# Score products of cosine attention in eight quarter tiles instead of two halves, from the second batch on

## The chip, the core and the metric

The kernel runs on one core of one Trainium2 chip, as one program. The core has a matrix engine (TensorE, PE in the profile, with its weight loads listed apart as PEld), a vector engine (DVE), a scalar engine that evaluates functions (ACT), GpSimd (POOL), and SyncE (SP), which here only issues transfers; transfers run on 16 DMA engines. The metric is the device time of one execution in microseconds, taken as the median of several runs.

## What is computed

Cosine attention, followed by two matrix products with a leaky ReLU between them. The reference, cut to what matters:

```python
# q, k, v: (8, 12, 448, 64): 8 batches, 12 heads, 448 positions, 64 features; tau = 0.1
q_n = q / (np.linalg.norm(q, axis=-1, keepdims=True) + 1e-06)
k_n = k / (np.linalg.norm(k, axis=-1, keepdims=True) + 1e-06)
scores = np.matmul(q_n, k_n.transpose(0, 1, 3, 2)) / tau
scores = scores - np.max(scores, axis=-1, keepdims=True)
attn = np.exp(scores)
attn = attn / (np.sum(attn, axis=-1, keepdims=True) + 1e-09)
x = np.matmul(attn, v)                  # heads laid side by side: (3584, 768)
h = x @ w_in                            # (768, 2048)
out = np.maximum(0.01 * h, h) @ w_out   # (2048, 768), float32
```

## The kernel before

**Tiling.** Work goes by slots. A slot `s` is a pair of heads of one batch, so there are six slots a batch and 48 in all. The normalised queries and keys of a slot, in bf16, lie transposed in `qkT[s]`: the 64 features of the first head in partitions 0 to 63, those of the second in 64 to 127; columns 0 to 447 are the queries and columns 512 to 895 are the first 384 keys. The last 64 keys of two neighbouring slots, an even one and the odd one behind it, share a tile: they stand in columns 448 to 511 of the two slots' `qkT`.

**Scores.** `key_tiles` (lines 240 to 264) gets a list of (slot, key tile) and works in two steps. First it issues the score products of all tiles on the list. A tile takes two neighbouring banks of `ps` (the eight accumulator banks of 512 columns), one for each head `a`. For key tiles 0 to 2 there are two products, one a head: 64 features by 128 keys as the weights, the 448 queries streaming past them. For key tile 3, called the strip tile in this document, there are four products of 64 by 64: two slots by two heads. All of them are on line 252, where the profile names them by rows and columns of their weights, 64\*128 and 64\*64. Then ACT takes the exponential of each whole tile, 128 partitions by 896 columns, into `pe` or `pr` (line 264). In this document one call's products of line 252 are called a run of scores.

**Sums and weighted values.** `attend` works on two slots. `totals` sums the exponentials over the keys by products with ones, and `products` multiplies them with the values; both go through `strip_products` (line 275), whose products are 128 by 32: four of them, one for each of four heads, write four strips of 32 partitions of one bank. With a call of `totals` and two of `products`, `attend` issues 48 such products. ACT turns the sums into reciprocals (lines 286 and 287), and DVE multiplies and writes `xT` (line 306).

**The two dense products.** `first` (line 324) multiplies `xT` with `w_in`, six products of 128 by 128 a group, and ACT applies the leaky ReLU (line 330). `second` (line 349) multiplies the result with `w_out`, 16 products a group; DVE copies it out (line 360) and SP sends it off.

**Order of the work.** The order is written out by hand. In the first batch (six slots) scores stand alone or in short runs between products that only keep PE occupied (`fill`, line 418), transposes on PE (line 209) and loads. From slot 6 on `deals["apart"]` is set to false, so that all eight banks are shared by all uses, and work of the batch before, two dense products in groups, is fed between the attention steps. The second batch's first slots have an order of their own (three runs of two full tiles and one strip tile alone), then come five units of a list called `opened`; every later batch has seven units of a list called `whole`. A unit is an optional `attend`, then one call of `key_tiles` with two or three tiles, then norms, loads and transposes for a slot ahead, then groups of dense products until the unit's share is done. After the last batch's scores only dense products are left.

`banks` hands out the banks that were used longest ago; a product that writes a bank waits until ACT or DVE has read what was in it.

Of the kernel before, what the change touches and what calls it, by code (L numbers as in the profile page):

```python
# [16 lines left out]
def kernel(  # L17
# [11 lines left out]
    B, H, S, D = q.shape  # L29
# [41 lines left out]
    ps = psp.tile([128, 8, 512], F32, name="ps")  # L71
    age = [0] * 8
    kept = {}
    deals = {"n": 0, "apart": True}

    def banks(count, keep=None):
        lo, hi = (0, 8) if not deals["apart"] else (0, 4) if count == 2 else (4, 8)
        x = min(
            (i for i in range(lo, hi, count) if not set(range(i, i + count)) & set(kept.values())),
            key=lambda i: max(age[i : i + count]),  # L80
        )
        deals["n"] += 1
        age[x : x + count] = [deals["n"]] * count
        if keep:
            kept[keep] = x
        return ps[:, x] if count == 1 else ps[:, x : x + count]
# [118 lines left out]
    qkT = {}  # L205
# [31 lines left out]
    def scores(s, kis):  # L237
        key_tiles([(s, ki) for ki in kis])

    def key_tiles(which):  # L240

        tiles = []
        for s, ki in which:
            sc = banks(2)
            tiles.append(sc)
            for i in range(2 if ki == 3 else 1):
                x = qkT[s - 1 + i] if ki == 3 else qkT[s]
                for a in range(2):
                    rows = slice(64 * a, 64 * a + 64)
                    out = sc[64 * i : 64 * i + 64] if ki == 3 else sc  # L250
                    c0, c1 = (448, 512) if ki == 3 else (512 + 128 * ki, 640 + 128 * ki)
                    nc.tensor.matmul(  # L252
                        out=out[:, a, :S], lhsT=x[rows, c0:c1], rhs=x[rows, 0:S],
                        start=True, stop=True,
                    )
        for (s, ki), sc in zip(which, tiles):
            if ki == 3:
                pr[s // 2] = prp.tile([128, 2, S], BF16, name="pr")
                dst = pr[s // 2]
            else:  # L260
                if s not in pe:
                    pe[s] = pep.tile([128, 3, 2, S], BF16, name="pe")
                dst = pe[s][:, ki]
            nc.scalar.activation(out=dst, in_=sc[:, :, :S], func=AF.Exp, scale=inv_tau)  # L264
# [50 lines left out]
    def chunk_cols(c):  # L315
        return (0, MAIN) if c % 2 == 0 else (MAIN, 512)
# [61 lines left out]
    for c in range(B):  # L378
        c0, n = chunk_cols(c)
# [82 lines left out]
    for s in range(NPAIR):  # L462
        j = s // 2 - 1 if s >= 2 else None
        even = s % 2 == 0
        n = s + 2 if s and s + 2 <= NPAIR + 1 else None
# [41 lines left out]
    def attend(j):  # L507
        totals(j)
        po = banks(2)
        for e in range(2):  # L510
            products(j, e, po[:, e])
        for e in range(2):
            scale(j, e)


    deals["apart"] = False
    s, j = NPAIR, NQ - 1
    attend(j)
    scores(s, (0, 1))
# [60 lines left out]
    for b in range(1, B):  # L580
# [3 lines left out]
        for i, (at, tiles, ahead) in enumerate(units):  # L584
# [3 lines left out]
            if at is not None:  # L588
                attend(b * NQ + at)
                load_v(b * NQ + at + 2)  # L590
            key_tiles([(b * NPAIR + p, ki) for p, ki in tiles])
            done = 0
            s = b * NPAIR + ahead if ahead else NSLOT
# [60 lines left out]
```

## Time and profile before

| | |
|---|---|
| median of 3 runs | 429.12 us (429.06 to 429.83) |
| span of the profiled execution, first to last instruction | 427.0 us |
| what lies around the span, against the median | 2.1 us |
| products of line 252 (scores) | 384, 46.1 us busy |
| products of line 275 (sums, values) | 1152 |
| products of line 324 (first dense product) | 768, 150.9 us busy |
| products of line 349 (second dense product) | 896, 151.9 us busy |
| ACT exponentials, line 264 | 144 of `pe` at 917 ns, 24 of `pr` at 925 ns |
| granted TensorE clock | 0.999 of full speed |

Busy time of PE is the time in which at least one product is under way. Products overlap: one takes 326 to 379 ns from start to end, while the next may start long before that end. What a product costs the engine is seen in the distance from its start to the next one's, not in its own duration.

### The profile page before, as it was taken

How to read it: one execution, taken by the hardware profiler on the slowest of the kernel's cores; microseconds unless marked ns; L12 is line 12 of the kernel's file. 1: busy time of each engine (PE TensorE's matmuls, PEld its weight loads, DVE VectorE, ACT ScalarE, POOL GpSimd, SP SyncE). 2: the span in 40 equal slices, each digit the busy share in tenths (PEclk: the TensorE clock that was granted, in tenths of full speed). 3: DMA queues.
4: the chain of work that ended last, by engine and by line, in shares of the span. 5: the costliest groups of instructions: out<-in, count | busy, mean ns of one | idle time of the engine just before them, and what ended most of it. 6: DMA issues, size and time to landing. Idle time of an engine off the chain costs nothing.

```text
span 427.0 us, 8670 instructions
## 1 busy us (share of the span) xinstructions
PE 416.3 (97%) x3333; PEld 208.7 (49%) x3333; DVE 188.1 (44%) x367; ACT 267.8 (63%) x494; POOL 138.4 (32%) x208
## 2 busy tenths in 40 slices
PE   8799999999999999999999999999999999999995
PEld 3234554544555555544455555544455555554563
DVE  5886767444363455343443554553343541220021
ACT  4997886667645796577663786568745686434300
POOL 3876544423134234513224142621424110000000
PEclk9999999999999999999999999999999999999999
DMA  6999999955458464943657456864547422010032
GB/s 153 218 221 220 222 218 194 257 131 125 88 122 168 101 135 102 212 118 82 129 109 148 100 126 126 176 116 128 96 105 138 77 60 41 38 74 2 0 75 74
DMA packets 102888, 53.65 MB, mean 126 GB/s; under 512 B 68928, under 2 KB 97856, under 8 KB 102848
## 3 DMA queue, kind: packets, MB, share of 16 engines
q1 hardware_dynamic: 76880, 40.75, 39.0%
q0 software_dynamic: 25056, 11.80, 21.7%
q10 hardware_dynamic: 912, 0.56, 0.4%
q8 instruction: 26, 0.43, 0.4%
q14 instruction: 14, 0.11, 0.1%
HBM read 45.61 MB, written 11.01 MB: 133 GB/s over the span
## 4 chain that ended last, share of the span: by engine, by line
PE 82%; DMA 12%; DVE 2%; ACT 1%; issue 1%; POOL 1%; SPq 0%; POOLq 0%; DVEq 0%
PE ps L349 33%; PE ps L324 31%; PE ps L275 11%; PE ps L252 7%; DMA w_out_sb<-in_moe_w_out_dram 6%; DMA q_h<-in_k_dram 4%; DMA q_h<-in_q_dram 3%; DVE qn L195 1%; ACT pe L264 1%; POOL sq L163 0%; DVE ss L174 0%; DVE r L191 0%; ACT ss L181 0%; ACT pr L264 0%; POOL v_b L142 0%
## 5 line engine op out<-in xcount | busy, mean ns | idle before, releaser
L349 PE MATMUL ps<-w_out_sb,hT 128*128 128x384 bf16 x896 | 151.9, 326 | 0.6 <-DMA w_out_sb<-in_moe_w_out_dram 0.6
L264 ACT ACTIVATE pe<-ps 128x896 bf16<-128x896 f32 x144 | 122.6, 917 | 47.5 <-PE ps L252 47.4
L324 PE MATMUL ps<-xT,w_in_sb 128*128 128x384 bf16 (+1 forms) x768 | 150.9, 353 | 0.0
L349 PEld LDWEIGHTS <-hT 128*128 128x128 bf16 x896 | 85.2, 98 | 63.5 <-issue 7.6
L324 PEld LDWEIGHTS <-w_in_sb 128*128 128x128 bf16 x768 | 73.2, 98 | 72.3 <-issue 7.0
L330 ACT ACTIVATE hT<-ps 128x384 bf16<-128x384 f32 (+1 forms) x128 | 65.1, 541 | 41.2 <-PE ps L324 40.4
L427 POOL CAST seen<-qn 128x1 f32<-128x1 bf16 x47 | 8.7, 184 | 202.1 <-DVE qn L195 202.1
L360 DVE COPY osb<-ps 128x384 f32<-128x384 f32 (+1 forms) x56 | 30.9, 552 | 97.4 <-PE ps L349 88.0
L174 DVE TENSOR_REDUCE ss<-sq 128x6 f32<-128x384 f32 (+1 forms) x95 | 56.1, 612 | 18.9 <-POOL sq L163 17.4
L163 POOL TENSOR_TENSOR sq<-q_h 128x512 f32<-128x512 f32 x46 | 48.0, 1044 | 6.5 <-DMA q_h<-in_k_dram 5.4
L252 PE MATMUL ps<-qkT 64*128 64x448 bf16 (+1 forms) x384 | 46.1, 358 | 3.2 <-ACT pe L264 1.4
L191 DVE RECIPROCAL r<-ss 128x14 f32<-128x14 f32 x48 | 11.5, 240 | 78.1 <-ACT ss L183 78.1
L306 DVE TENSOR_TENSOR xT<-ps,rb 128x448 bf16<-128x448 f32 x48 | 27.9, 619 | 30.0 <-ACT rb L287 29.9
L163 POOL TENSOR_TENSOR sq<-k_h 128x384 f32<-128x384 f32 x47 | 39.0, 829 | 5.6 <-DMA k_h<-in_k_dram 5.6
L275 PE MATMUL ps<-pe,v_b 128*32 128x448 bf16 x576 | 35.6, 353 | 0.0
L195 DVE TENSOR_TENSOR qn<-q_h,r 128x512 bf16<-128x512 f32 x48 | 34.1, 710 | 2.2 <-DVE r L191 0.7
L286 ACT ACTIVATE rb<-ps 128x448 f32<-128x448 f32 x24 | 13.1, 544 | 34.6 <-PE ps L275 34.5
L252 PEld LDWEIGHTS <-qkT 64*128 64x128 bf16 (+1 forms) x384 | 12.8, 96 | 37.7 <-issue 30.7
L195 DVE TENSOR_TENSOR qn<-k_h,r 128x384 bf16<-128x384 f32 x48 | 27.3, 569 | 0.0
L264 ACT ACTIVATE pr<-ps 128x896 bf16<-128x896 f32 x24 | 22.2, 925 | 0.0
L275 PEld LDWEIGHTS <-v_b 128*32 128x32 bf16 x576 | 15.2, 97 | 11.9 <-issue 0.4
L150 POOL DMA_DIRECT2D v_rem<-in_v_dram x32 | 20.6, 648 | 0.0
(39 smaller groups left out, 183.1 us busy)
## 6 DMA issues: line engine op xcount, KB each, us to landing
q_h<-in_q_dram SPq DMA_DIRECT2D x48, 192.0 KB, 3.1
k_h<-in_k_dram SPq DMA_DIRECT2D x46, 192.0 KB, 3.1
out_dram<-osb SPq DMA_DIRECT2D x30, 192.0 KB, 3.2
v_b<-in_v_dram POOLq DMA_DIRECT2D x24, 192.0 KB, 5.4
out_dram<-osb SPq DMA_DIRECT2D x12, 384.0 KB, 2.8
w_in_sb<-in_moe_w_in_dram POOLq DMA_DIRECT2D x4, 768.0 KB, 11.0
w_out_sb<-in_moe_w_out_dram POOLq DMA_DIRECT2D x2, 1536.0 KB, 22.5
q_h<-in_q_dram SPq DMA_DIRECT2D x48, 32.0 KB, 3.8
```

The source lines that it names most:

```text
L150: gp.dma_start(out=vrb[b % 2][lo : lo + 64, :, g], in_=r[g])
L163: eng.tensor_tensor(sq, x, x, op=ALU.mult)
L174: nc.vector.tensor_reduce(o.rearrange("p (h t) -> p h t", h=2), sqs[s][i], axis=AX.X, op=ALU.add)
L195: nc.vector.tensor_tensor(qn[s][:, lo:hi], x.rearrange("p h t d -> p t h d"), r[:, r0 : r0 + 2 * nt].rearrange("p (h t) -> p t h", h=2) .u ...
L252: nc.tensor.matmul(out=out[:, a, :S], lhsT=x[rows, c0:c1], rhs=x[rows, 0:S], start=True, stop=True,)
L264: nc.scalar.activation(out=dst, in_=sc[:, :, :S], func=AF.Exp, scale=inv_tau)
L275: nc.tensor.matmul(out=x[32 * g : 32 * g + 32, :S], lhsT=weights(g, ki) if ki < 3 else rem(g), rhs=pe[s][:, ki, a, :] if ki < 3 else pr[j] ...
L306: nc.vector.tensor_tensor(xT[m][:, 2 * jj + e, half * S : (half + 1) * S], pos.pop((j, e))[:, :S], rbs[j], op=ALU.mult,)
L324: nc.tensor.matmul(out=pm[:, :n], lhsT=w_in_sb[:, kt, m * 128 : (m + 1) * 128], rhs=xT[c // 2][:, kt, c0 : c0 + n], start=(kt == 0), stop= ...
L330: nc.scalar.activation(out=hT[c][:, m, :n], in_=pm[:, :n], func=AF.Prelu, alpha=0.01)
L349: nc.tensor.matmul(out=po2[:, :HALF], lhsT=hT[c][:, m, ts * 128 : (ts + 1) * 128], rhs=w_out_sb[:, m, half * HALF : (half + 1) * HALF], st ...
L360: nc.vector.tensor_copy(out=o[:, half * HALF : half * HALF + cut], in_=po2[:, :cut])
```

## The change

Each key tile's scores are split by key columns. With a width of 32, every tile, the strip tile too, becomes eight products of 64 features by 32 keys (four column parts by two heads), each with its own weight load; they write the same two banks, each 32 partitions of one bank. The streamed queries, the exponential behind it, the tiles and their order stay. In the first batch the width stays 128, which gives the same products as before, the strip tile's four of 64 by 64 included. From slot 6 on the width is 32.

```diff
-    deals = {"n": 0, "apart": True}
+    deals = {"n": 0, "apart": True, "width": 128}
...
-            for i in range(2 if ki == 3 else 1):
-                x = qkT[s - 1 + i] if ki == 3 else qkT[s]
+            width = deals["width"] if ki < 3 else min(deals["width"], 64)
+            for p in range(0, 128, width):
+                x, c0 = (qkT[s - 1 + p // 64], 448 + p % 64) if ki == 3 else (qkT[s], 512 + 128 * ki + p)
                 for a in range(2):
                     rows = slice(64 * a, 64 * a + 64)
-                    out = sc[64 * i : 64 * i + 64] if ki == 3 else sc
-                    c0, c1 = (448, 512) if ki == 3 else (512 + 128 * ki, 640 + 128 * ki)
                     nc.tensor.matmul(
-                        out=out[:, a, :S], lhsT=x[rows, c0:c1], rhs=x[rows, 0:S],
-                        start=True, stop=True,
+                        out=sc[p : p + width, a, :S], lhsT=x[rows, c0 : c0 + width],
+                        rhs=x[rows, 0:S], start=True, stop=True,
                     )
...
     deals["apart"] = False
+    deals["width"] = 32
     s, j = NPAIR, NQ - 1
```

## The prediction

> **What bounds the kernel now.** I read the page's busy shares first, then the chain of waits, then the busy time by stage, then single stretches of the timeline.
>
> ```profile
> PE 416.3 (97%) x3333; PEld 208.7 (49%) x3333; DVE 188.1 (44%) x367; ACT 267.8 (63%) x494; POOL 138.4 (32%) x208
> PE 82%; DMA 12%; DVE 2%; ACT 1%; issue 1%; POOL 1%; SPq 0%; POOLq 0%; DVEq 0%
> ```
>
> The first line is busy time, the second the shares of the chain that ended last. Both name TensorE (PE). The stages say where (length of the stretch, then busy microseconds of each engine):
>
> ```profile
> 37.00:74.00 37.00, 36.43 (x335) 19.52 (x328) 26.18 (x49) 28.46 (x57) 19.29 (x28) 1.00 1.27 214
> 74.00:380.00 306.00, 306.00 (x2498) 154.53 (x2496) 130.27 (x251) 199.95 (x366) 95.12 (x142) 1.00 0.56 119
> ```
>
> From 74 to 380 us PE is busy 306.00 of 306.00 us; ScalarE (ACT) has 106 us spare there, VectorE (DVE) 176. The chain, in order of time, turns to PE for good here:
>
> ```profile
> 49.69 23.96 DMA w_out_sb<-in_moe_w_out_dram
> 73.69 2.77 PE ps L349 x16
> ```
>
> So before 73.69 us the second w_out load sets the time, and PE waits for it once:
>
> ```profile
> 72.39 0.74 PE L252 MATMUL ps<-qkT 64*128 64x448 bf16 x6
> 73.69 0.50 PE L349 MATMUL ps<-w_out_sb,hT 128*128 128x384 bf16 x2 [0.57 <-DMA w_out_sb<-in_moe_w_out_dram]
> ```
>
> What the score products cost PE before 73.69 us changes this wait (about 0.6 us) and not the end; what they cost behind it, to the last scores at 373 us, goes into the end one for one.
>
> A busy PE does not say what a product costs, since products overlap. The cost is in the starts of the timeline:
>
> ```profile
> 202.15 0.74 PE L275 MATMUL ps<-pe,v_b 128*32 128x448 bf16 x12
> 202.71 0.36 PE L275 MATMUL ps<-pr,v_rem 128*32 128x448 bf16 x4
> 202.90 0.74 PE L275 MATMUL ps<-pe,v_b 128*32 128x448 bf16 x12
> 203.47 0.36 PE L275 MATMUL ps<-pr,v_rem 128*32 128x448 bf16 x4
> 203.76 0.74 PE L252 MATMUL ps<-qkT 64*128 64x448 bf16 x6
> 204.44 0.39 PE L324 MATMUL ps<-xT,w_in_sb 128*128 128x512 bf16 x1
> ```
>
> Columns are start, extent and count. Twelve 128x32 products (three rounds of four strips) take 202.71 - 202.15 = 0.56 us: a round of four passes in the time of one product of 448 columns. The trace's own starts, to the nanosecond, give 189 ns from round to round, and 3 to 4 ns between the four of a round (hence an extent of 0.36 us for four that last 352 ns each). 448 columns in about 187 ns is what streaming takes: a 512-wide L324 product follows the last at 216 ns, a 384-wide L349 product at 163, so 2.4 columns per ns and 2 to 3 ns. The six score products of 203.76 are three tiles of two: starts at 0 and 3, 199 and 203, 389 and 392 ns. Two products of 64 rows run together too.
>
> The shape costs something where it **changes**. The round of 203.47 ends its stream at 203.66, yet the scores begin at 203.76. Over all runs of scores, the time from the end of the last stream to the next start, beyond the streaming, is 95 to 99 ns on entry from 128x128 or from 128x32, and 94 ns on leaving 64x128. A third such change lies inside runs that hold a strip tile (ki = 3):
>
> ```profile
> 212.32 0.86 PE L252 MATMUL ps<-qkT 64*128 64x448 bf16 x8
> 213.12 0.34 PE L349 MATMUL ps<-w_out_sb,hT 128*128 128x384 bf16 x1
> ```
>
> Eight products, still three tiles, but 0.80 us from start to the next line's start against 0.68 for the run of six. The starts: the third tile, four 64x64 products, comes 282 ns after the second where 190 would do, 95 ns for the change from 64x128 to 64x64, its four start within 10 ns, and leaving it costs 119 ns instead of 94.
>
> **The change part by part.** It adds 840 products with as many weight loads (147 tiles by eight is 1176, against 126 by two and 21 by four, 336). It moves no step and issues no DMA; queues, banks and waits stay in their order. All tiles of a run now have one shape, 64x32.
>
> *Removed:* the change of shape inside a run, 95 ns, and the dearer exit.
>
> *One tile's round.* No row shows eight tiles of 64x32 together. The nearest: four of 128x32 in 189 ns (four column strips together) and four of 64x64 within 10 ns (two row halves by two column halves together). Lower bound 189 ns, as these; upper bound 378, as two rounds of four. I take 189, because both divisions are seen to run together, and once jointly.
>
> *The spread of the eight starts.* 3.3 ns each by the rows of four: 7 x 3.3 = 23 ns from first to last, where two have 3 to 4 now. Later rounds follow their own strip, so this counts once a run. Lower bound 3 ns.
>
> *Entry and exit.* Entry 95 to 98 ns in every direction seen, a change of rows alone (128x128 to 64x128) among them, so I take 98 and no saving next to L275. Exit lies between 94 (64x128) and 119 ns (64x64); I take 98, which L275 shows for 32 columns after 48 products. I put the 25 ns of 64x64 down to its weight loads: every first round shows some of them (a lone 64x128 tile leaves at 105, and first rounds of 128x32 last 199 ns against 189), but four loads of 32 columns show 10 ns, four of 64 show 25, and in a run of several tiles the last round's loads are long done.
>
> *A run, from its first start to the next line's start.* Three tiles: 199 + 189 + 23 + 187 + 98 = 696 ns. Before: 674 ns with three full tiles, 798 ns with two full tiles and a strip tile. Two tiles: 199 + 23 + 187 + 98 = 507, before 608 (the run at 76.40: one full, one strip).
> Behind 73.69 us: 24 runs of three full tiles, four in each of the six later batches, at +22 ns: +0.53 us. 18 runs with a strip tile at -102: -1.84. One at -101: -0.10. **Sum: -1.41 us.** The eight runs before 73.69 add up to +0.03 us, which comes off the wait on w_out; without that cover they would cost 0.03.
>
> *What else moves.* ACT's exponentials start about 20 ns later after a tile's first product (the last of eight starts later); L264 is hidden by PE's following products, and by 106 us of ACT's idle time. If it weren't, it would cost 43 x 20 ns = 0.9 us.
>
> **The sum.** The profiled execution spans 427.0 us; the runs have a median of 429.12, so 2.1 us lie around the span, which nothing here touches. 425.6 + 2.1 = **427.7 us**. With the bounds of spread (20 ns less), exit (4 less to 21 more) over 43 runs: -2.5 to -0.5 us, or 426.6 to 428.6. The doubtful round is a rival.
>
> **Rivals.**
>
> *No change.* If the 119 ns exit belongs to dividing rows and columns at once, every run pays 21 ns more: -1.41 + 0.90 = -0.5 us, 428.6. For it: the only row with both divisions has it. Against: the 10 ns that first rounds show at 32 columns, which point to the loads.
>
> *Slower, by the supply of instructions.* A run of 24 products wants 24 loads and 24 products dealt within 411 ns, 17.9 ns a pair; the L275 stretches need only 189 / 4 = 47 ns a pair. If PE's sequencer deals a pair in X, a run lasts 23X + 285; today's 43 runs average 724, so it turns into a loss from X = 19 ns. No row excludes that: the quickest supply seen behind a wait is at 29.25 us, 18 loads and products in 0.30 us, 33 ns a pair. At 33: three tiles last 1044, so 24 x 370 + 18 x 246 ns + 0.2 = 13.5 us, and the early runs 2.4 less 0.6 of wait; 444.4. Against: where a score product had waited 0.3 us (28.17), the next load and product followed within 6 ns, and rounds begin 4 products and 4 loads in 13 ns, so work seems to stand ready behind the array. The Trainium skill, "TensorE: Matmul & The Clock Gate" (its opening table), gives PE's queue a depth of 64; a run's 48 instructions would then fit. No run here shows that depth.
>
> *Slower, two rounds a tile.* Three tiles last 696 + 567. 24 x 589 + 18 x 465 + 277 ns = 22.8 us, early runs 3.0 after the wait: 454.9. For it: no row has more than four products together. Against: 128x32 and 64x64 both run all they have.
>
> *Slower, a floor between starts.* If products never started closer than some floor F, whatever their strip, a run would last 23F + 285, as above. The rows bound F by 3 to 4 ns (the strips of L275, no cost) and 56 ns (L209's transposes on the whole array, 53 of it streaming). Half way, 30 ns, a run of 24 lasts 975: 24 x 301 + 18 x 177 + 127 ns = 10.5 us, early runs 1.4 after the wait, so 441.0. Against: starts 3 to 4 ns apart in every L275 round, so a floor could only come with eight tiles. The Trainium skill, same page, in "Wait — 56ns, not 53.3ns?", says that starts never come closer than about 25 ns however few the columns; an estimate by it is +6.3 us, 435.4. The trace's 3 to 4 ns between strips disagree, and the trace decides.
>
> *The change isn't made.* The width is set ahead of every later score; 1 in 100.
>
> **How the numbers follow.** Forecast 0.66; no change 0.13; supply 0.09; two rounds 0.07; floor 0.04; not made 0.01. A measurement of this kernel tells about 0.2% (0.86 us) from no change. Faster 0.66, same 0.14 (with the change not made), slower 0.20. The likeliest gives 427.7. The range runs from 426.6, the forecast's lower bound, to 429.6, past the case of no change; the three slower rivals, 0.20, are left out.
>
> **What would show it.** L252 with 1176 products of 64x32 and 48 of the old shapes; runs of 24 with starts at 0 to 23, 199 and 388 ns and 0.70 us to the next line, with or without a strip tile; no gap inside; the w_out wait unchanged at 0.6 us; PE still busy throughout from 74 us, and its last product 1.4 us earlier. Wrong if: a round's second four start 189 ns after the first four (two rounds); starts at even steps over 19 ns (supply or a floor); exits near 119 (no change); or PE idle with ACT as releaser.

## The result and the profile after

The changed kernel took 427.55 us in the median (15 runs, 426.87 to 429.58), the kernel before 429.20 in the same comparison (15 runs, 428.28 to 429.83): a ratio of 0.9970, 95% interval 0.9958 to 0.9982. Faster by 0.3%, as forecast (427.7). The profiled execution spans 425.7 us, where the sum said 425.6.

Busy time by engine and the chain that ended last, from the page of the changed kernel:

```profile
PE 413.7 (97%) x4156; PEld 210.4 (49%) x4173; DVE 187.9 (44%) x367; ACT 267.4 (63%) x494; POOL 138.0 (32%) x208
PE 82%; DMA 13%; ACT 1%; DVE 1%; issue 1%; POOL 1%; SPq 0%; POOLq 0%; DVEq 0%
```

840 more weight loads (4173 against 3333) and nearly as many more products on record (4156; a few product records are missing), yet PE is busy 2.6 us less (2.3 us in the second profile of this kernel, which has all 4173 products), and it still sets the end. The products of the score line, which has moved from 252 to 251, by shape (count, busy time, mean of one, then idle time before):

```profile
L251 PE MATMUL ps<-qkT 64*32 64x448 bf16 x1176 | 37.7, 353 | 0.0
L251 PE MATMUL ps<-qkT 64*128 64x448 bf16 x36 | 5.8, 356 | 3.2 <-ACT pe L263 1.4 <-ACT ss L182 1.2 <-ACT ss L181 0.3
L251 PE MATMUL ps<-qkT 64*64 64x448 bf16 x12 | 1.1, 373 | 0.0
```

All 1176 new products came without a wait ahead of any. The timeline around the same two runs as before, one of three full tiles, one with a strip tile (start, extent, count):

```profile
203.14 0.36 PE L274 MATMUL ps<-pr,v_rem 128*32 128x448 bf16 x4
203.43 0.76 PE L251 MATMUL ps<-qkT 64*32 64x448 bf16 x24
204.12 0.82 PE L323 MATMUL ps<-xT,w_in_sb 128*128 128x512 bf16 x2
...
212.01 0.76 PE L251 MATMUL ps<-qkT 64*32 64x448 bf16 x24
212.70 1.15 PE L348 MATMUL ps<-w_out_sb,hT 128*128 128x384 bf16 x6
```

Both runs now have 24 products and the same 0.69 us from first start to the next line's start; before they had 0.68 and 0.80. The trace's starts in nanoseconds, typical of the 42 runs of three tiles: the first round at 0, 3, 6, 10, 13, 16, 20, 23, the second from 200 to 222, the third from 389 to 411, the next line at 693 to 695. The 43 runs behind the w_out wait sum to 1.50 us less than before, and what lies between them to 0.10 us less.

The end of PE's wait on w_out, from which the prediction counted, came later than before:

```profile
72.53 0.76 PE L251 MATMUL ps<-qkT 64*32 64x448 bf16 x24
74.03 0.50 PE L348 MATMUL ps<-w_out_sb,hT 128*128 128x384 bf16 x2 [0.75 <-DMA w_out_sb<-in_moe_w_out_dram]
```

From here to the last product's start PE takes 346.82 us by the trace's starts, before 348.41: 1.60 us less. In this execution w_out landed 0.34 us later (74.03 against 73.69 us), which leaves the 1.3 us between the spans. This stretch, called PE's stretch below, is the sharp gauge: its three measurements in the changed kernel are 346.82, 346.81 and 346.81 us, while whole runs of one kernel differ by over 1 us.

### The profile page after: what moved, and what is told of

It reads as the page before. It is cut to its first block, busy times and chain, and to the rows that moved or that the text cites. A ratio compares the mean times of both kernels' runs of the same rounds, so it can differ in the third digit from the quotient of the medians.

```text
span 425.7 us, 10343 instructions
## 1 busy us (share of the span) xinstructions
PE 413.7 (97%) x4156; PEld 210.4 (49%) x4173; DVE 187.9 (44%) x367; ACT 267.4 (63%) x494; POOL 138.0 (32%) x208
## 3 DMA queue, kind: packets, MB, share of 16 engines
HBM read 45.61 MB, written 11.01 MB: 133 GB/s over the span
## 4 chain that ended last, share of the span: by engine, by line
PE 82%; DMA 13%; ACT 1%; DVE 1%; issue 1%; POOL 1%; SPq 0%; POOLq 0%; DVEq 0%
PE ps L348 33%; PE ps L323 31%; PE ps L274 11%; PE ps L251 7%; DMA w_out_sb<-in_moe_w_out_dram 6%; DMA q_h<-in_q_dram 3%; DMA q_h<-in_k_dram 3%; DMA k_h<-in_k_dram 1%; DVE qn L195 1%; ACT pe L263 1%; POOL sq L163 0%; DVE ss L174 0%; DVE r L191 0%; ACT ss L181 0%; ACT pr L263 0%
## 5 line engine op out<-in xcount | busy, mean ns | idle before, releaser
L263 ACT ACTIVATE pe<-ps 128x896 bf16<-128x896 f32 x144 | 122.6, 918 | 48.9 <-PE ps L251 48.8
L174 DVE TENSOR_REDUCE ss<-sq 128x6 f32<-128x384 f32 (+1 forms) x95 | 56.2, 612 | 19.5 <-POOL sq L163 17.9
L251 PE MATMUL ps<-qkT 64*32 64x448 bf16 (+1 forms) x1224 | 44.7, 353 | 3.2 <-ACT pe L263 1.4
L251 PEld LDWEIGHTS <-qkT 64*32 64x32 bf16 (+1 forms) x1224 | 14.5, 90 | 30.9 <-issue 23.8
L263 ACT ACTIVATE pr<-ps 128x896 bf16<-128x896 f32 x24 | 22.2, 926 | 0.0
```

The source lines that it names most:

```text
L174: nc.vector.tensor_reduce(o.rearrange("p (h t) -> p h t", h=2), sqs[s][i], axis=AX.X, op=ALU.add)
L251: nc.tensor.matmul(out=sc[p : p + width, a, :S], lhsT=x[rows, c0 : c0 + width], rhs=x[rows, 0:S], start=True, stop=True,)
```

## The experiments

Twelve runs: ten edits, and the changed kernel twice more. The stretch is from one profile each, the time a median against runs of the kernel before on the same chip.

| kernel | full tiles / strip tiles | PE's stretch, us (against before) | time, us (before) | ratio, 95% interval |
|---|---|---|---|---|
| before | 64x128 / 64x64 | 348.41 | | |
| changed, again | 64x32 / 64x32 | 346.81 (-1.60) | 427.61 (428.92) | 0.9969 (0.9954 to 0.9985) |
| changed, third time | 64x32 / 64x32 | 346.81 (-1.60) | 427.58 (429.28) | 0.9957 (0.9945 to 0.9970) |
| `w64` | 64x64 / 64x64 | 346.85 (-1.57) | 426.68 (428.92) | 0.9947 (0.9929 to 0.9965) |
| `full32` | 64x32 / 64x64 | 349.19 (+0.78) | 429.98 (428.92) | 1.0032 (1.0016 to 1.0049) |
| `strip32` | 64x128 / 64x32 | 348.41 (0.00) | 428.67 (428.93) | 0.9992 (0.9981 to 1.0002) |
| `strip_mid` | before, strip tile in the middle | 350.33 (+1.92) | 431.26 (428.93) | 1.0044 (1.0031 to 1.0058) |
| `mixed` | 64x32 in runs with a strip tile alone | 346.38 (-2.03) | 426.58 (428.92) | 0.9953 (0.9936 to 0.9970) |
| `mixed64` | 64x64 in runs with a strip tile alone | 346.41 (-2.01) | 427.08 (429.28) | 0.9943 (0.9931 to 0.9956) |
| `early32` | 64x32 ahead of the wait alone | 348.41 (0.00) | 429.21 (429.28) | 0.9999 (0.9988 to 1.0011) |
| `split2` | 64x32 in two halves of the queries | 347.14 (-1.27) | 428.79 (428.93) | 0.9995 (0.9982 to 1.0008) |
| `split4` | 64x32 in four quarters | 359.42 (+11.01) | 446.11 (428.93) | 1.0389 (1.0373 to 1.0405) |
| `w64_split8` | 64x64 in eight parts | 357.97 (+9.56) | 444.45 (429.28) | 1.0338 (1.0322 to 1.0354) |

**Is it the narrow tile or the single shape?** First every tile in 64x64:

```diff
-    deals["width"] = 32
+    deals["width"] = 64
```

> Every tile from the second batch on as four 64x64 products. My theory, that the gain comes from one shape throughout a run and that a first round shows its weight loads by their width (10 ns at 32 columns, 25 at 64): no shape change inside runs, first to second round about 214 ns, later rounds 189, exit 95 ns, so a run of three tiles lasts about 695 ns from its first start to the next line's, as with 64x32, and the time is that of the changed kernel within 0.2 us, 1.4 to 1.6 us under before. Rival, that dividing rows and columns into 64x64 has the dear exit of 119 ns wherever it ends: runs of 720 ns, only 0.4 us under before. Rival, that narrow products are quicker in themselves: the gain halves or goes.

```profile
210.93 0.76 PE L251 MATMUL ps<-qkT 64*64 64x448 bf16 x12
211.62 0.66 PE L348 MATMUL ps<-w_out_sb,hT 128*128 128x384 bf16 x3
```

Half as many products, the same run of 694 ns. Its starts: second round at 213 ns, third at 402, exit 95 ns. So the first round does show 14 ns more of its loads than with 32 columns (213 against 199 or 200), and a run's end doesn't show 119 ns. The saving is that of the changed kernel to 0.03 us in the stretch. The time came out about 0.7 us lower than that accounts for; more on that below.

Then the two halves of the change, one at a time. Quarter tiles for the full tiles alone:

```diff
-            width = deals["width"] if ki < 3 else min(deals["width"], 64)
+            width = deals["width"] if ki < 3 else 64
```

> Full tiles as eight 64x32 products, strip tiles left as four 64x64: undoes the part of the change that makes the run uniform. My theory: the change of shape inside the run stays (95 ns), runs with a strip tile last about 820 ns (before 798, changed kernel 694), runs of full tiles 694 (before 674); behind the w_out wait 24 x 20 + 18 x 22 ns + 20 ns, so about 0.9 us slower than before, some 430.1 us. Rival, that the 64x32 full tiles bring the gain: still about 1.5 us faster than before.

```profile
213.98 0.89 PE L251 MATMUL ps<-qkT 64*32 64x448 bf16 x20
214.80 1.47 PE L348 MATMUL ps<-w_out_sb,hT 128*128 128x384 bf16 x8
```

This is a run with a strip tile (the merged row carries the first shape's name): 818 ns, expected 820. Runs of full tiles last 694. The kernel is slower than before: the 64x32 tiles in themselves cost 20 ns a run.

And quarter tiles for the strip tiles alone:

```diff
-            width = deals["width"] if ki < 3 else min(deals["width"], 64)
+            width = 128 if ki < 3 else min(deals["width"], 64)
```

> Full tiles as two 64x128 products, strip tiles alone as eight 64x32. My theory: the shape still changes inside the run, so a run with a strip tile lasts 482 + 23 + 187 + 105 = 797 ns against 798 before, and the time is that of before within 0.2 us. Rival, that quarter tiles help the strip tile by themselves: runs under 750 ns and over 0.8 us faster than before.

```profile
212.55 0.86 PE L251 MATMUL ps<-qkT 64*128 64x448 bf16 x12
213.35 0.50 PE L348 MATMUL ps<-w_out_sb,hT 128*128 128x384 bf16 x2
```

798 ns, the old value to the nanosecond: the exit falls from 119 to 105, the spread of eight starts takes it back, and the shape still changes inside the run. Neither half gains; both together do.

**Doubling the suspected cost.** The kernel before, with the strip tile in the middle, so that the shape changes twice inside the run:

```diff
-        (None, [(2, 0), (2, 1), (1, 3)], 5),
+        (None, [(2, 0), (1, 3), (2, 1)], 5),
...
-        (None, [(3, 2), (4, 0), (3, 3)], 7),
+        (None, [(3, 2), (3, 3), (4, 0)], 7),
...
-        (None, [(5, 1), (5, 2), (5, 3)], None),
+        (None, [(5, 1), (5, 3), (5, 2)], None),
```

> The kernel before, with the strip tile in the middle of its run instead of last, so that the shape changes twice inside the run: doubles the suspected cost. My theory: the second tile starts at 292 ns, the third at about 608, the run lasts about 903 ns against 798, 18 runs of these behind the w_out wait: 1.9 us slower than before, about 431.1 us. Rival, that the strip tile is dear because of its four products and not of the change beside it: run still about 800 ns and no difference.

```profile
214.12 0.97 PE L252 MATMUL ps<-qkT 64*128 64x448 bf16 x8
215.02 1.15 PE L349 MATMUL ps<-w_out_sb,hT 128*128 128x384 bf16 x6
```

905 ns, expected 903. The same products, banks and exponentials, and 18 more changes of shape make PE's stretch 1.92 us longer. With `strip32` this settles the mechanism: a change of shape costs some 95 to 107 ns, whichever way it goes, and the edit took one out of each of 19 runs.

**A version that beats both.** As full tiles lose 20 ns a run by the change, only runs with a strip tile need it:

```diff
+        mixed = any(ki == 3 for _, ki in which)
...
-            width = deals["width"] if ki < 3 else min(deals["width"], 64)
+            width = min(deals["width"], 64 if ki == 3 else 128) if mixed else 128
```

> 64x32 only in runs that hold a strip tile; runs of full tiles keep two 64x128 products. My theory: 18 runs lose 104 ns and one 103, runs of full tiles stay at 674 instead of 694, so PE's stretch from the w_out wait to the last product is 1.98 us shorter than before and 0.4 to 0.5 us shorter than in the changed kernel: about 427.2 us against 427.6. Rival, that the shape of one run tells on the next one (a first 64x32 after long 64x128 work costs more): entries over 98 ns and no gain on the changed kernel.

```profile
202.48 0.74 PE L252 MATMUL ps<-qkT 64*128 64x448 bf16 x6
203.15 5.35 PE L324 MATMUL ps<-xT,w_in_sb 128*128 128x512 bf16 x24
...
211.04 0.76 PE L252 MATMUL ps<-qkT 64*32 64x448 bf16 x24
211.73 1.47 PE L349 MATMUL ps<-w_out_sb,hT 128*128 128x384 bf16 x8
```

0.67 and 0.69 us: each run has its cheaper form. The same with 64x64 instead of 64x32 in those runs (`width` set to 64 in place of 32):

> Full tiles as 64x128 in runs of full tiles; runs that hold a strip tile wholly in 64x64. Candidate for the best version, with 252 fewer products than the same with 64x32. My theory: one shape a run is what counts, so runs of 673 and 694 ns as in the mixed kernel before it; PE's stretch behind the w_out wait 346.4 us (before 348.4, changed kernel 346.8); 2.0 us under before. Rival, that fewer products help by themselves: stretch under 346.2 us.

Again 694 ns in runs with a strip tile, and PE's stretch is 2.0 us shorter than before, 0.4 shorter than in the changed kernel. Both beat the kernel before clearly. Against the changed kernel the times lie 1.0 and 0.5 us lower on the same chip, but the intervals overlap: that they beat it is shown by the stretch, not by the times. The two comparison runs of the changed kernel expected and gave this:

> The changed kernel once more on the same chip as the three others, for comparison: 1.6 us less PE time behind the w_out wait than before, ratio 0.996 to 0.997; runs of 694 ns.

> The changed kernel on the same chip as the three others, for comparison: PE's stretch behind the w_out wait 346.8 us; ratio to before 0.996 to 0.997.

The stretch came out as expected both times. The second ratio, 0.9957, fell just under the band given, with an interval that covers it.

**Is early PE time covered?** The narrow products in the first batch and up to the w_out wait, the old ones behind it:

```diff
-    deals = {"n": 0, "apart": True, "width": 128}
+    deals = {"n": 0, "apart": True, "width": 32}
...
-    deals["width"] = 32
...
+            if b > 1 or i == len(units) - 1:
+                deals["width"] = 128
```

> 64x32 only in the first batch and in the second batch's runs ahead of the w_out wait, the old products behind it: tests that PE's time ahead of that wait is covered. My theory: PE's stretch behind the wait as before (348.4 us), the time that of before within 0.3 us, as early runs change by 20 ns each at most and the loads decide. Rival, that early scores are on the path to the loads: the time moves by over 0.8 us, one way or the other.

The time is that of before (0.9999) and the stretch is 348.41 us, as the theory said. The test is weak, though: 25 early runs at 20 ns are 0.5 us at most, no more than the interval resolves, and the wait that was to cover them wasn't there in the profiled execution:

```profile
73.43 0.76 PE L251 MATMUL ps<-qkT 64*32 64x448 bf16 x24
74.13 0.50 PE L348 MATMUL ps<-w_out_sb,hT 128*128 128x384 bf16 x2
```

Here PE came to this point 1.0 us later than in the profile of before, and w_out was there already. That isn't this kernel's doing alone: up to the third run of scores, at 14 us, the profiles agree to 0.5 us, and around 16 to 20 us, in the first batch, some executions fall behind by about 0.8 us, the unchanged first batch of `strip32` and of the changed kernel's third profile among them. The granted clock (third figure from the end) shows how. From 16 to 18 us, first `strip32`, which fell behind, then `w64`, which didn't:

```profile
16.00:18.00 2.00, 2.00 (x10) 0.40 (x9) 0.79 (x2) 1.42 (x3) 2.00 (x4) 0.50 1.17 241
16.00:18.00 2.00, 1.81 (x17) 0.69 (x15) 1.22 (x4) 2.00 (x4) 2.00 (x4) 1.00 1.16 231
```

In `strip32` the three stretches of 2 us from 14 us on have 0.74, 0.50 and 0.91, together some 3.4 us at half clock. Nine of the fourteen profiled executions have such a time there; those of before, `w64`, `mixed` and two of the changed kernel don't. What sets it off is open. Leaving out the two kernels with 96 products a run, the seven with it get past the w_out load at 73.7 to 75.0 us, the five without at 72.9 to 74.0. PE's wait on w_out was anywhere from nothing to 0.78 us (`full32`), and in three of the seven it was still over 0.6 us, so there the load had come later too (25.1 us after its issue at 49.9 us in `full32`, 24.0 us after 49.7 in before). Time lost in the first batch is therefore not simply covered by the wait. It didn't matter for the change, because its early runs add up to nearly nothing.

The same clock goes with a good part of what strayed in `w64`: none of its eight runs has a granted clock under 0.997 over the whole span, while 12 of the 30 runs of the kernel before on that chip have 0.996 or less, and these have a median of 429.41 us against 428.51 for the other 18. Against those 18, `w64` is 1.8 us faster, where the stretch gives 1.57.

**Where would the supply of instructions bind?** Each 64x32 product in two halves of 224 query columns, then in four of 112 (line 251's loop inside a loop over the parts):

```diff
+            parts = 2 if deals["width"] == 32 else 1
+            n = S // parts
+            for q0 in range(0, S, n):
...
-                        out=sc[p : p + width, a, :S], lhsT=x[rows, c0 : c0 + width],
-                        rhs=x[rows, 0:S], start=True, stop=True,
+                            out=sc[p : p + width, a, q0 : q0 + n], lhsT=x[rows, c0 : c0 + width],
+                            rhs=x[rows, q0 : q0 + n], start=True, stop=True,
```

> The changed kernel with each 64x32 product cut into two of 224 query columns: 48 products and loads a run, 12 ns a pair wanted. My theory, that products and loads stand ready and eight tiles run at once with no floor between starts: half rounds 96 ns apart, a run of about 700 to 710 ns against 694, about 0.5 us slower than the changed kernel, 428.0 us. Rivals: supply at X ns a pair gives a run of 47 X + 190; at 17.9 ns that is 1030 ns and 14 us more, at 33 ns 1740 ns and 45 us more. A floor of 25 ns: 1365 ns and 29 us more.

```profile
212.23 0.77 PE L254 MATMUL ps<-qkT 64*32 64x224 bf16 x48
212.93 0.99 PE L351 MATMUL ps<-w_out_sb,hT 128*128 128x384 bf16 x5
```

701 ns with 48 products, half rounds 96 ns apart: 12 ns a pair is supplied with ease. The stretch is 0.33 us longer than in the changed kernel, where about 0.5 was expected; against before the time should then be 1.27 us lower and is 0.14 lower (0.9995). In the profiled execution 0.43 us of the missing 1.1 lie ahead of the stretch, which begins at 74.12 us instead of 73.69; where the other runs lose theirs isn't shown, nor whether the additional instructions cost it.

> The changed kernel with each 64x32 product cut into four of 112 query columns: 96 products and loads a run, about 6.1 ns a pair wanted. It looks for the place at which the supply of instructions does bind. If starts can go on at 3.3 ns a pair: quarter rounds 49 ns apart, a run of about 720 ns, 1 us more than the changed kernel. If a sequencer or the weight loads (a load must be done within a quarter round) bind at X ns a pair: a run of 95 X + 140; at 10 ns 1090 ns and 17 us more, at 17.9 ns 1840 ns and 49 us more.

```profile
88.59 1.03 PE L254 MATMUL ps<-qkT 64*32 64x112 bf16 x96
89.56 0.66 PE L351 MATMUL ps<-w_out_sb,hT 128*128 128x384 bf16 x3
```

Here it binds: 0.96 us in most runs of three tiles, 1.02 to 1.10 us in ten of the 42. The first 32 products start in bursts of eight, quarter rounds 49 ns apart as wanted, up to 182 ns. The next starts at 248, and from there on products come evenly, 8.3 ns apart (248, 256, 264, 272, ...), but for a step of 34 ns at the 64th and the 96th. The 43 runs account for 12.6 of the 18.5 us by which it is slower than the changed kernel (446.11 against 427.58 us); most of the others lie in the early part, as PE gets past the w_out load only at 80.13 us. To see whether the pace is that of the instructions, of the weight loads or of a round, 64x64 products in eight parts of 56 columns:

```diff
-            parts = 4 if deals["width"] == 32 else 1
+            parts = 8 if deals["width"] == 64 else 1
...
-    deals["width"] = 32
+    deals["width"] = 64
```

> 64x64 throughout, each product cut into eight of 56 query columns: 96 products and loads a run, about 6.5 ns a pair wanted. Asks what bound the four-way split of 64x32, whose first 32 pairs ran at the wanted pace and the others at 8.3 ns a pair after a pause of 66 ns. Theory A, the dealing of instructions behind a queue of some 64 places: again about 32 pairs at the wanted pace, then 8.3 ns a pair, a run of 900 to 980 ns. Theory B, the weight loads: 64 columns take twice as long as 32, so about 16 ns a pair, from the first rounds on, a run over 1500 ns. Theory C, a time per round on one tile (66 ns from round to round there): four pairs a round, so again 16 ns a pair.

```profile
89.08 1.00 PE L254 MATMUL ps<-qkT 64*64 64x56 bf16 x96
90.01 1.31 PE L351 MATMUL ps<-w_out_sb,hT 128*128 128x384 bf16 x7
```

929 ns, and again evenly 8.3 ns apart in the latter part, with loads of twice the width and four pairs to a round. Theories B and C are out, and A's pace holds; that it is the dealing of instructions is what is left, not something a trace shows. Its queue of 64 places is not as plain: the even pace sets in after 32 pairs in one kernel and after some 60 in the other, whose rounds of four came at 31 to 32 ns. Yet the starts fit one supply for both. In the median of the undisturbed runs the 56th product starts at 445 ns here and at 439 in `split4`, the 69th at 579 and 573, the 96th at 813 and 824. Rounds of 31 to 32 ns take 7.9 ns a product, hardly quicker than 8.3, and they started later (the 33rd product at 274 ns, in `split4` at 247), so the supply falls behind them only about there. The late onset doesn't speak against theory A, and doesn't show a queue of 64 either.

## Why the prediction was right, step by step

**PE's stretch behind w_out is the bound.** Borne out: in every kernel whose products aren't cut along the queries, the time against before follows the stretch within 0.7 us, in most within 0.4, and PE's wait on ACT stayed at 1.4 us, all of it in the first batch. What didn't hold is that time ahead of w_out comes off a wait of about 0.6 us: that wait isn't fixed, the load itself comes at different times, and `split4` loses 6 us ahead of it, which no wait covers. `early32` is too weak to decide. The change was spared, as its early runs add up to 0.03 us.

**The change of shape inside the run.** Priced at 95 ns and confirmed from four sides (`w64`, `full32`, `strip32`, `strip_mid`). The Trainium skill, "TensorEngine Tiling (Array Packing)", in "Key Properties", says that a change of tiling mode, and not of the tile alone, drains TensorE; the trace agrees, with 94 to 99 ns on entry to a run and 94 to 119 on leaving one.

**The round.** 189 ns was taken between the bounds of 189 and 378. The rounds are 189 ns apart: eight tiles of 64x32 do run together. The rival of two rounds a tile is out.

**The spread.** 23 ns, as measured (0 to 23).

**Entry and exit.** Taken at 98 each, measured 96 and 95. This is where the sum was off: a run lasts 694 ns and not 696, and entry costs 96: 4 ns over 43 runs, 0.17 us, which with rounding makes -1.60 us of the sum's -1.41. The rival of no change, with 119 ns at every exit, is out: `w64` shows 95 at the end of runs that divide rows and columns at once, and 213 ns to the second round, so what 64x64 shows above others comes with the first round's loads, as was assumed.

**The total.** That the profiled span of 425.7 us met the sum's 425.6 is partly luck: the stretch fell by 0.19 us more than the sum said, and w_out came 0.34 us later. The 2.1 us around the span set one execution's span against the median of others; within the single runs listed with both, time and span differ by 1.7 to 1.9 us. The forecast doesn't hang on it, since 427.7 is the median of 429.12 less 1.41.

**The supply of instructions and the floor.** Both would have shown as even starts over 19 ns; starts within a round are 3 to 4 ns apart. The supply was the better founded doubt: `split4` and `w64_split8` show it at 8.3 ns a pair once the first products are through, where the change needed 17.9 and the rival was priced at 33. The Trainium skill's depth of 64 for PE's queue ("TensorE: Matmul & The Clock Gate", its opening table) agrees with the 64 loads and products that `split4` started at the wanted pace; the other kernel doesn't contradict it and doesn't show it.

**ACT.** L263's exponentials stay hidden: PE waits for them no more than before.

## What to carry to other kernels

Price a small product by the distance between starts and by the changes of array shape around it, not by its duration or by their number: here 18 more products in a run of full tiles cost 20 ns, and a single change of shape costs 95 to 107 ns. Give a run of products one shape, the widest that all of it can take, and narrow only those runs that would otherwise change shape inside; whether these then are 64x64 or 64x32 made no difference here. When a step of 0.3% is to be judged, a stretch of the trace in which one engine is never idle resolves it to 0.02 us, while whole runs differ by more than the effect.

## What the runs showed of the hardware that was not expected

A pair of load and product can be dealt to PE every 8.3 ns over dozens of pairs; that pace was the same for 32 and for 64 columns of weights. In ten of the 42 runs of three tiles behind w_out, in either kernel, PE stood still once for some 80 to 145 ns more. In `split4`, ahead of 66 us and with the transfers at their busiest, it stood still twice inside a run for much longer, which no other engine explains:

```profile
57.09 0.83 PE L254 MATMUL ps<-qkT 64*32 64x112 bf16 x74
58.88 0.33 PE L254 MATMUL ps<-qkT 64*32 64x112 bf16 x22 [0.96 <-issue]
...
62.57 0.89 PE L254 MATMUL ps<-qkT 64*32 64x112 bf16 x81
65.35 0.29 PE L254 MATMUL ps<-qkT 64*32 64x112 bf16 x15 [1.89 <-issue]
```

`w64_split8` did so behind the same products, the 74th of one run and the 81st of the next:

```profile
59.13 0.37 PE L254 MATMUL ps<-qkT 64*64 64x56 bf16 x22 [0.89 <-issue]
...
65.87 0.31 PE L254 MATMUL ps<-qkT 64*64 64x56 bf16 x15 [2.15 <-issue]
```

In both kernels there are exactly 128 products, each with its load, from one of these stops to the other. The profile gives issue as the releaser. The transfers of the queue that it calls instruction point to late loading of instructions (number, MB and share, first before, then `split4`):

```profile
q8 instruction: 26, 0.43, 0.4%
q8 instruction: 60, 0.98, 0.9%
```

`split4` has 34 more of them, of 16384 bytes each, for 8736 more loads and products: one for every 257, and the two stops are 256 apart. Each of the four stops ended 2.2 to 2.4 us after one of these transfers began (at 56.64 and 63.00 us in `split4`, 56.80 and 63.45 in `w64_split8`), though most such transfers end no stop. No run changes how instructions are loaded, so the cause stays likely and not shown.

The longer stop was followed by a lower granted clock, here by stage in `split4` (the third figure from the end of each line):

```profile
37.00:66.00 29.00, 26.15 (x619) 16.25 (x608) 18.10 (x33) 22.33 (x45) 15.15 (x21) 1.00 1.26 219
66.00:70.00 4.00, 4.00 (x20) 2.12 (x19) 0.20 (x1) 1.35 (x4) 0.00 (x0) 0.59 1.24 229
70.00:74.00 4.00, 4.00 (x118) 2.70 (x117) 2.96 (x7) 0.55 (x1) 1.36 (x3) 0.98 0.93 127
```

From 66 to 70 us the granted clock was 0.59, and products of 384 columns came 320 ns apart instead of 163; in `w64_split8` it was 0.57, with the same 320 ns. Behind the shorter stop, at 58 to 59 us, the clock stayed at 1.00 in both.
